# Spreading the rounding of the second MLP weights and stretching the first half of the first MLP chunk

## Chip, cores, metric

One core of a Trainium2 chip. The metric is the device time of one launch in microseconds (us); the median of several executions is given. TensorE is called PE, VectorE DVE, ScalarE ACT and GpSimd POOL, as in the profile.

## The reference

```
scores = q @ k.T / 8                       # 8 x 8 heads, 576 x 576, head size 64
thresh = max(scores, axis=-1) - 0.02
attn   = softmax(where(scores >= thresh, scores, -1e9))
x      = (attn @ v), heads side by side    # 4608 tokens x 512
out    = relu(x @ w_in)**2 @ w_out         # w_in 512 x 2048, w_out 2048 x 512
```

## The kernel before

Attention goes in 160 steps: a pair of heads and one block of 128 queries (the fifth block of a visit, the half block, has 64 queries of both heads). The MLP goes in 12 chunks of 384 tokens. A chunk's work waits in a queue and is dealt out between the attention's parts by a rate; its first half is 32 `mlp_in` parts, its second 24 `mlp_out` parts. The weights come as 64-bit floats and are rounded on the chip in 32 pieces: 0 to 15 are w_in, 16 to 31 w_out.

One piece passes three engines:

```python
        if stage == 0:      # ScalarE, twice
            nc.scalar.activation(out=e, in_=hi.bitcast(FP32), func=AF.Copy, scale=2.0 ** -112)
            nc.scalar.activation(out=d, in_=lo, func=AF.Copy, scale=2.0 ** -52)
        elif stage == 1:    # VectorE, lines 116, 117, 119
            nc.vector.tensor_scalar(out=tu, in0=hi, scalar1=0x80000000, ...)
            nc.vector.scalar_tensor_tensor(out=tu, in0=eu, scalar=3, in1=tu, ...)
            nc.vector.tensor_scalar(out=eu, in0=tu, scalar1=0xFF800000, ...)
        elif stage == 2:    # GpSimd, line 121
            nc.gpsimd.tensor_tensor(out=d, in0=d, in1=e, op=ALU.mult)
        else:               # GpSimd, line 123
            nc.gpsimd.tensor_tensor(out=weight_piece(i)[1], in0=t, in1=d, op=ALU.add)
```

The softmax's start has, after each pair of row maxima, three tiny operations of 128 x 2 elements:

```python
        for u in range(n):
            nc.vector.tensor_reduce(out=mx[:, u:u + 1], in_=sc[u][:, :, 0:HALF], ...)            # line 184
        nc.vector.tensor_scalar(out=bias, in0=mx, scalar1=-SCALE, scalar2=None, op0=ALU.mult)    # 185
        nc.vector.tensor_scalar(out=thr, in0=mx, scalar1=ntau8, scalar2=None, op0=ALU.add)       # 186
        nc.vector.tensor_tensor(out=z, in0=thr, in1=mx, op=ALU.is_gt)                            # 189
```

The loop (cut), with the rate and the table of pieces:

```python
    def rate(s):
        have = sum(x[0] for x in waiting)
        best = 1e9
        for e in sorted(chunk_at) + [NST + 2]:
            if e > s:
                best = min(best, have / (e - s))
                have += CHUNK_US * len(chunk_at.get(e, ()))
        return best
    ...
        if s <= min(chunk_at) - 2:                 # min(chunk_at) is 13
            x = int(visits[n][1].index(i) != 1)
        else:
            x = 1 if n < 2 * HP else 2
        pieces.append(min(x, left))
    ...
    for s in range(NST + 3):
            if now:
                round_weights(now[0], 0)
            scores(n, i)
            if now or early():
                exponents(n, i)
            if now:
                round_weights(now[0], 1)
                round_weights(now[0], 2)
            ...  # transposes of the next q and k, mix, a quarter of the MLP work
        for part in range(3):
            turn(*steps[s - 1], part)      # transposes of the last step's weights
            ...  # threshold after part 0, divide after part 1, a quarter of the MLP work
            if now:
                end_rounding(now[0])       # the add, and the load of the piece after next
            for p in now[1:]:              # a second piece: all of it here
                for stage in range(3):
                    round_weights(p, stage)
                end_rounding(p)
```

## Time and profile before

| | before |
|---|---|
| median, range (us) | 1628.0 (1627.86 to 1628.01), 3 executions |
| span of the profiled execution | 1625.4 |
| PE / DVE / POOL busy | 96% / 43% / 31% |

A stage's row in the profile gives its bounds, its length, the busy us and number of instructions of each engine, the clock that TensorE was granted (1.00 is full) and the DMA share. Everything from step 39 on is full of TensorE work, so what can be won or lost is TensorE's time before it: idle, or run at half clock.

### The profile page before, as it was taken

The page shows a single profiled execution, that of the slowest core. Times are in us where ns is not written, and L with a number is a line of the kernel's source. Part 1 is how long each engine was busy: PE and PEld are TensorE (multiplying, and loading weights), DVE is VectorE, ACT ScalarE, POOL GpSimd, SP SyncE. Part 2 cuts the span into 40 slices and gives each one's busy share as a digit, 9 for nine tenths or more (in the row PEclk, how much of TensorE's full clock was granted, in tenths as well). Part 3 has the DMA queues.
Part 4 walks back from the last instruction along what each step waited for, and adds up shares of the span by engine and source line. Part 5 has one row for each costly group of instructions (what it writes and reads, how often), then busy time and mean ns, then how long its engine had stood idle before and what let it go on. Part 6 is the DMA issues. An engine that isn't in the chain of part 4 may idle for free.

```text
span 1625.4 us, 18644 instructions
## 1 busy us (share of the span) xinstructions
PE 1561.2 (96%) x6464; PEld 851.8 (52%) x6464; DVE 696.0 (43%) x1833; ACT 556.3 (34%) x1157; POOL 503.6 (31%) x655
## 2 busy tenths in 40 slices
PE   5789779999999999999999999999999999999998
PEld 3455435555555455555555455555556455555453
DVE  6778994444344334444434344343434434320000
ACT  3555543333333233333333333233234233221010
POOL 4457771232232132132133133123124123212030
PEclk9889889999999999999999999999999999999999
DMA  6446330210210110120111110120111020000000
GB/s 149 93 111 145 91 83 7 57 23 7 48 32 7 35 23 1 35 51 1 35 29 23 35 29 0 35 44 8 29 35 22 7 57 1 14 13 0 20 1 20
DMA packets 224190, 59.29 MB, mean 36 GB/s; under 512 B 215392, under 2 KB 215392, under 8 KB 224096
## 3 DMA queue, kind: packets, MB, share of 16 engines
q1 hardware_dynamic: 224064, 58.10, 16.3%
q8 instruction: 52, 0.85, 0.2%
q14 instruction: 42, 0.34, 0.1%
q0 software_dynamic: 32, 0.00, 0.0%
HBM read 48.63 MB, written 9.44 MB: 36 GB/s over the span
## 4 chain that ended last, share of the span: by engine, by line
PE 89%; DVE 7%; SPq 1%; issue 1%; ACT 0%; POOL 0%; DMA 0%; DVEq 0%; ACTq 0%; POOLq 0%
PE o L286 30%; PE h L270 29%; PE s L180 11%; PE x_ps L254 10%; PE w_ps L227 7%; DVE st L184 2%; DVE w L207 2%; DVE cv L117 1%; PE w_ps L231 1%; SPq L136 1%; DVE cv L119 1%; DVE cv L116 1%; DVE st L185 1%; DVE st L186 0%; ACT w L196 0%
## 5 line engine op out<-in xcount | busy, mean ns | idle before, releaser
L270 PE MATMUL h<-xT,w_in_sb 128*128 128x384 f32 x1536 | 549.7, 493 | 0.0
L286 PE MATMUL o<-w_out_sb,g 128*128 128x512 f32 x1152 | 540.9, 599 | 0.0
L216 POOL TENSOR_SCALAR w<-w,st 128x576 f32<-128x576 f32 x288 | 238.0, 835 | 565.8 <-DVE st L210 550.2
L184 DVE TENSOR_REDUCE st<-s 128x1 f32<-128x576 f32 x288 | 206.8, 753 | 417.8 <-PE s L180 417.8
L207 DVE SCALAR_TENSOR_TENSOR w<-s,st,w 128x576 f32<-128x576 f32 x288 | 224.8, 814 | 315.9 <-ACT w L196 315.8
L270 PEld LDWEIGHTS h<-xT,w_in_sb 128*128 128x128 f32 x1536 | 271.6, 191 | 162.4 <-issue 30.8
L286 PEld LDWEIGHTS o<-w_out_sb,g 128*128 128x128 f32 x1152 | 200.9, 190 | 189.1 <-issue 187.7
L228 ACT COPY wT<-w_ps 128x384 f32<-128x384 f32 x384 | 180.8, 482 | 316.4 <-PE w_ps L227 315.4
L276 POOL TENSOR_TENSOR g<-r 128x384 f32<-128x384 f32 x192 | 159.6, 831 | 367.9 <-ACT r L274 366.6
L227 PEld LDWEIGHTS w_ps<-ident,w 128*128 128x128 f32 x1152 | 150.5, 145 | 157.1 <-issue 109.0
L180 PE MATMUL s<-kT,qT 64*128 64x288 f32 x1024 | 182.7, 448 | 41.8 <-DVE w L207 32.9
L196 ACT ACTIVATE w<-s,st 128x576 f32<-128x576 f32 x288 | 200.2, 745 | 56.7 <-DVE st L185 56.6
L227 PE MATMUL w_ps<-ident,w 128*128 128x128 f32 x1152 | 189.2, 282 | 14.1 <-ACT wT L228 10.3
L274 ACT ACTIVATE r<-h 128x384 f32<-128x384 f32 x192 | 94.4, 492 | 250.0 <-PE h L270 240.3
L254 PE MATMUL x_ps<-wT,vs 128*64 128x192 f32 (+1 forms) x1280 | 177.6, 426 | 0.0
L180 PEld LDWEIGHTS s<-kT,qT 64*128 64x128 f32 x1024 | 102.9, 194 | 131.3 <-issue 92.2
L254 PEld LDWEIGHTS x_ps<-wT,vs 128*64 128x64 f32 x1280 | 89.1, 142 | 82.9 <-issue 70.7
L257 ACT COPY xT<-x_ps 128x384 f32<-128x384 f32 (+1 forms) x64 | 25.4, 397 | 242.2 <-PE x_ps L254 242.2
L121 POOL TENSOR_TENSOR cv<-cv 128x512 f32<-128x512 f32 x32 | 40.7, 1273 | 53.3 <-DVE cv L119 45.2
L290 ACT COPY osb<-o 128x512 f32<-128x512 f32 x36 | 21.1, 586 | 104.0 <-PE o L286 101.8
L180 PE MATMUL s<-kT,qmid 128*128 128x288 f32 x128 | 38.5, 426 | 4.1 <-DVE w L207 4.1
L186 DVE TENSOR_SCALAR st<-st,ntau 128x2 f32<-128x2 f32 (+1 forms) x160 | 39.4, 246 | 0.0
(37 smaller groups left out, 504.0 us busy)
## 6 DMA issues: line engine op xcount, KB each, us to landing
ql<-in_q_dram SPq DMA_DIRECT2D x144, 72.0 KB, 2.7
kl<-in_k_dram SPq DMA_DIRECT2D x144, 72.0 KB, 2.7
vs<-in_v_dram SPq DMA_DIRECT2D x72, 128.0 KB, 2.5
out_dram<-osb SPq DMA_DIRECT2D x36, 256.0 KB, 2.1
area<-in_moe_w_in_dram SPq DMA_DIRECT2D x16, 512.0 KB, 4.1
area<-in_moe_w_out_dram SPq DMA_DIRECT2D x16, 512.0 KB, 3.7
vs<-in_v_dram SPq DMA_DIRECT2D x72, 16.0 KB, 2.4
ntau<-in_tau_dram POOLq DMA_DIRECT2D x1, 0.5 KB, 3.3
```

Of the source, the lines that this page charges most:

```text
L180: nc.tensor.matmul(sc[u][:, half, 0:HALF], lhsT, kT[rows, at:at + HALF], start=True, stop=True)
L184: nc.vector.tensor_reduce(out=mx[:, u:u + 1], in_=sc[u][:, :, 0:HALF], axis=AX.XY, op=ALU.max)
L196: nc.scalar.activation(out=w[:, u, :].rearrange("p (h k) -> p h k", h=2), in_=sc[u][:, :, 0:HALF], func=AF.Exp, bias=st[:, 1, u:u + 1], sc ...
L207: nc.vector.scalar_tensor_tensor(out=wu, in0=sc[u][:, :, 0:HALF], scalar=thr[:, u:u + 1], in1=wu, op0=ALU.is_ge, op1=ALU.mult, accum_out=s ...
L216: nc.gpsimd.tensor_scalar(out=w[:, u, :], in0=w[:, u, :], scalar1=z[:, u:u + 1], scalar2=rcp[:, u:u + 1], op0=ALU.add, op1=ALU.mult)
L227: nc.tensor.transpose(ps[:, n, :], w.rearrange("p u k -> p (u k)")[:, c * P:(c + 1) * P], ident)
L228: nc.scalar.copy(wT[:, 3 * part:3 * part + 3, cols], ps[:, 0:3, :])
L254: nc.tensor.matmul(ps[u * D:(u + 1) * D, 0:nq], vs[n % 2][:, u * (NBLK + 1) + c, :], wT[:, cw, cols], start=(c == 0), stop=(c == NBLK))
L270: nc.tensor.matmul(h, w_in_sb[:, c, f * P:(f + 1) * P], xT[:, c, at:at + TCH], start=(c == 0), stop=(c == NMC - 1))
L274: nc.scalar.activation(out=r, in_=h, func=AF.Relu)
L276: nc.gpsimd.tensor_tensor(out=gs[j, f], in0=r, in1=r, op=ALU.mult)
L286: nc.tensor.matmul(o, gs[j, f][:, t * P:(t + 1) * P], w_out_sb[:, f, :], start=(f == 0), stop=(f == NFT - 1))
```

## The change

Its intent: two pieces a step crowd VectorE in steps 20 to 27, so round one a step (two only in the half block), and slow the first half of chunk 0 so that its second half, which reads w_out, starts only when w_out is nearly rounded.

```diff
     def rate(s):
+        if s < out_from:
+            return sum(x[0] for x in waiting if x[1] is mlp_in) / (out_from - s)
         have = sum(x[0] for x in waiting)
@@
-            x = 1 if n < 2 * HP else 2
+            x = 2 if n >= 2 * HP and i == NBLK else 1
         pieces.append(min(x, left))
@@
+    out_from = next(s for s in range(NST) if sum(pieces[:s]) >= n_pieces - 2)
```

`out_from` comes out as 32.

## The prediction

> **What bounds the kernel now.** I read the busy table first, then the 40 slices, then the stretches around the MLP's first chunk, then the waits and single instructions inside the slow stretch.
>
> ```profile
> PE 1561.2 (96%) x6464; PEld 851.8 (52%) x6464; DVE 696.0 (43%) x1833; ACT 556.3 (34%) x1157; POOL 503.6 (31%) x655
> ...
> PE   5789779999999999999999999999999999999998
> ...
> DVE  6778994444344334444434344343434434320000
> ...
> POOL 4457771232232132132133133123124123212030
> PEclk9889889999999999999999999999999999999999
> ```
>
> TensorE is 96% busy, so nothing that only makes another engine cheaper can help after about 280 us (slice 7 on). The weak place is the first six or seven slices of 40.6 us: PE shows 7 in slices 4 and 5 (162 to 244 us) while DVE shows 9, and the clock is not full. That is where the second weights are rounded.
>
> I cut the trace at the first score matmul of chosen attention steps. There are 160 steps (pair of heads, block of queries); the first MLP chunk is admitted at step 13, the next at step 39. Step 13 begins at 99.66 us, step 20 at 150.68, step 28 at 233.14, step 39 at 311.99. The columns are length, busy us of the engines, PE clock, DMA share.
>
> ```profile
> core 0: us, PE busy (x) PEld busy (x) DVE busy (x) ACT busy (x) POOL busy (x), PEclk, DMA share, GB/s
> 99.66:150.68 51.02, 48.52 (x242) 29.17 (x242) 41.90 (x97) 27.64 (x61) 37.12 (x45) 0.96 0.63 143
> 150.68:233.14 82.46, 63.68 (x262) 35.35 (x263) 76.75 (x138) 41.62 (x84) 62.14 (x60) 0.88 0.43 105
> 233.14:311.99 78.85, 75.23 (x335) 39.90 (x334) 44.48 (x118) 28.86 (x61) 21.55 (x29) 0.97 0.08 19
> 311.99:1625.40 1313.41, 1309.22 (x5357) 706.61 (x5355) 462.02 (x1306) 413.50 (x869) 337.98 (x464) 1.00 0.11 23
> ```
>
> Steps 13-19 (one rounded piece each) take 7.3 us each, steps 20-27 (two pieces) 10.3, steps 28-38 (none) 7.2. In the second row DVE is 93% busy and PE 77%: VectorE bounds it. In the last row PE is 99.7% busy, and the change leaves that row's work alone. So only 212.3 us (51.0 + 82.5 + 78.9) are in play. The same stretch shows what two pieces a step do:
>
> ```profile
> ACT cv L113 <- POOL w_out_sb L123: 29.8, 7, 5.3
> ...
> PE w_ps L227 <- ACT wT L228: 10.3, 3, 4.1
> ...
> PE s L180 <- DVE w L207: 5.8, 4, 4.2
> ```
>
> ScalarE stands still seven times before the first conversion of a piece, because the two rounding buffers are still held by GpSimd; being in order, it then delivers its PSUM copies late, PE idles 3 to 4 us, and comes back slow:
>
> ```profile
> 187.48 0.90 PE L227 MATMUL w_ps<-ident,w 128*128 128x128 f32 x3 [4.11 <-ACT wT L228]
> 188.17 2.77 PE L270 MATMUL h<-xT,w_in_sb 128*128 128x384 f32 x4
> 190.74 2.13 PE L180 MATMUL s<-kT,qmid 128*128 128x288 f32 x4
> ...
> 196.19 1.56 PE L270 MATMUL h<-xT,w_in_sb 128*128 128x384 f32 x4
> ```
>
> The same four h matmuls take 2.77 us just after the idle 4.11 us, and 1.56 us (1.30 from start to start in a row of them) once warm.
>
> **What the Trainium skill says.** "TensorE: Matmul & The Clock Gate", Part 1 (the HAM clock gate): the array runs at half clock after an idle window of about 3.4 us and at full clock after a busy one. The trace agrees: 2.77 against 1.56 us above, and a mean clock of 0.88 in the second stretch. "SBUF — State Buffer", Who interferes with whom: VectorE and GpSimd share one pair of SBUF ports as an exclusive lock that some VectorE forms take, and the loser waits out the whole instruction. The trace agrees: the mask of a piece (line 116) takes 0.41 us alone but 1.50 us at 163.74, 175.49, 185.94, exactly beside GpSimd's 1.27 us multiply or add. I found no page needed for the DMA: the loads run four pieces ahead.
>
> **The change part by part.** No instruction is added or removed: 32 pieces, 768 + 576 MLP matmuls, the same attention. Only their places move.
>
> Rounding. Nine pieces are done before step 13 in both. Before, 7 in steps 13-19 and 16 in steps 20-27. After: 7 in 13-19; then one per step, two in the last block of a visit (steps 24 and 29), until the 23 are out in step 33. So 14 pieces in steps 20-31, 2 in 32-33.
>
> MLP. The 32 first-half pieces of chunk 0 (1.30 us of PE each) used to go out 17 in steps 13-19, 15 in 20-25, and its 24 second-half pieces (1.72 us each) in steps 26-38. Now the new rate spreads the first half evenly up to step 32: 12 pieces in 13-19, 20 in 20-31; then all 24 second-half pieces fall in 32-38, three or four per step. I followed the fill rule step by step for these counts. From step 39 both kernels stand alike within one piece.
>
> *Steps 13-19.* Same pieces on DVE, 5 fewer h parts, 6.5 us less on PE. But the loop here is score matmul, reduce, rounding, threshold, next score: for a full block, from reduce at 124.72 to the reciprocal's end at 130.70 is 6.0 us; a half block with its transposes 130.61 to 136.83, 6.2 us; and 0.93 to 1.28 us of waiting for PE per pair: 13.4 us per pair. Less PE work and a few less GpSimd squarings barely shorten it. 51.0 becomes 50.
>
> *Steps 20-31, now 12 steps.* A full block with one piece costs 6.0 us and a score round trip of about 1.0: 7.0. The step that transposes the next q and k adds 2 x 0.75: 8.5. The last block of a visit with two pieces: 6.2 - 1.5 + 2.3 = 7.0 on DVE, but PE has 1.1 of scores, 3.4 of mixing, some 2.1 of h and 1.15 of transposes, 7.7; so 7.7. Its second piece hides the next round trip, so block 0 after it costs 6.0. Steps 20-23: 7.0 + 8.5 + 7.0 + 7.0 = 29.5; 24-28: 7.7 + 6.0 + 8.5 + 7.0 + 7.0 = 36.2; 29-31: 7.7 + 6.0 + 8.5 = 22.2. Sum 87.9. I add 2 for cold spells: PE carries only 26 us of h and about 39 of attention here (72%), so idle spots of 1.5 to 2.5 us recur and some may drop the clock. 90.
>
> *Steps 32-38.* PE: 24 x 1.72 = 41.3, scores 8.1, transposes 7.5, mixing 3.4 + 1.8: 62.1, plus 2 for the first steps: 64. DVE's 7 x 4 us and two pieces lie beside it.
>
> Sum 50 + 90 + 64 = 204 against 212.3: a gain of 8. With the 1628.0 measured: 1620. The gain is small because VectorE's work is unchanged: the pieces cost 53.2 us of DVE in this stretch, 2.3 each, of which 2.1 or less is their own when no port is contested.
>
> **The rivals.** (a) *Nothing gained, or a little lost.* The work moved off PE in steps 13-31 must be done later, where PE is full: steps 32-38 cost 64 for 7 steps, against 50 (7 x 7.2) before, and VectorE's loop with a single piece leaves a hole at each round trip that a second piece used to fill. For it: steps 13-19 already run at 7.3 us with one piece and hold 3 us more h per pair than they will. If steps 20-31 cost 8.2 each and the clock drops often, 51 + 98 + 65 = 214: 1630. Against: the 7.3 include cold spells at step 13, which took 10.4 us.
> (b) *Full repair.* All stalls of two-piece steps vanish, contention halves, and steps 20-31 go at 6.5: 48 + 78 + 62 = 188, a gain of 24: 1604. For it: steps 28-38 before took 7.2 with more PE work. Against: DVE's own work in steps 13-31 is 127 us uncontended (13 full blocks of 4.33, 6 half of 2.69, 7 transposes of 1.5, 21 pieces of 2.1), and in steps 20-31 alone there remain the round trips.
> (c) *A late weight.* Second-half pieces start at step 32 with 30 pieces rounded; the last two rows are first read by the eighth piece, in step 34, a step after the last is rounded. I expect no wait. If each were a few us: 1625.
>
> **Range and chances.** Centre 1620; half of the weight within 5 us. Rival (a) gives the upper side, a mild form of (b) the lower: 1611 to 1629. Faster by over 2% needs 32.6 us out of 212; the PE work in it alone is about 168 (82 of MLP and 86 of attention at warm rates) and VectorE's bound leaves even less, so 0.02. Slower by over 2% would need steps 13-38 to average 9.4 us, 0.01. Within 2%: 0.97.
>
> **What would show it.** Of the profile after: step 20 begins at about 150, step 32 at about 240, step 39 at about 304, and from there to the end again 1313 us. DVE busy in steps 20-31 near 85%, not 93%; ScalarE's wait for GpSimd before line 113 shrinks from 29.8 us to under 5; PE idles of over 3 us in these steps fall from four to at most two; the line 116 mask's mean over the run drops below its 605 ns. I am wrong if step 32 begins after 248 (rival a, then look for idle PE before scores and a clock below 0.88) or before 230 (rival b), or if out matmuls wait for weights (rival c), or if the stretch from step 39 differs by more than 3 us.

## The result, and the profile after

| | before | after |
|---|---|---|
| median (us) | 1627.93 (1625.67 to 1628.01), 4 executions | 1624.26 (1623.77 to 1625.47), 4 executions |
| ratio after / before | | 0.9982, 95% interval 0.9965 to 0.9999 |

A ratio here is the mean time of one kernel's fast executions over the mean of the other's in the same rounds, so it is not quite the ratio of the medians. The unaltered changed kernel ran twice more on other occasions, with five rounds each: 1623.57 us, ratio 0.998 (0.9967 to 0.9994), and 1623.73 us, ratio 0.9981 (0.9967 to 0.9995). It is a gain of about 3 us where 8 were predicted: the direction was right, the size less than half. Measured by a bound of 2%, the two kernels count as the same, and so does every run below; what follows reads the 95% intervals.

The slices of the changed kernel:

```profile
PE   5788879999999999999999999999999999999999
...
DVE  6778775434444343444334344343434434320000
...
PEclk9789889999999999999999999999999999999999
```

The dip of TensorE is now an 8, 8, 8, 7 and longer; VectorE's two 9s are gone. The same stages, cut at steps 13, 20, 32 and 39:

```profile
core 0: us, PE busy (x) PEld busy (x) DVE busy (x) ACT busy (x) POOL busy (x), PEclk, DMA share, GB/s
99.41:150.31 50.90, 43.53 (x223) 26.19 (x223) 41.42 (x97) 27.27 (x59) 34.37 (x43) 0.93 0.60 138
150.31:248.15 97.84, 78.04 (x368) 46.08 (x368) 78.77 (x173) 50.17 (x103) 62.82 (x68) 0.88 0.38 91
248.15:310.60 62.45, 62.45 (x250) 31.46 (x250) 31.24 (x86) 22.27 (x45) 19.83 (x24) 1.00 0.11 23
310.60:1623.70 1313.10, 1309.18 (x5356) 706.69 (x5354) 461.18 (x1302) 413.27 (x868) 337.64 (x463) 1.00 0.11 23
```

In the kernel before, step 32 begins at 264.6 by the score matmuls of its trace, and its steps 20 to 31 were

```profile
150.68:264.61 113.93, 92.67 (x391) 50.42 (x392) 94.91 (x179) 51.80 (x106) 72.45 (x72) 0.90 0.32 79
```

The stages beside their predicted lengths:

| steps | before | predicted | after, first profile | second and third |
|---|---|---|---|---|
| 13 to 19 | 51.0 | 50 | 50.9 | 50.5, 50.7 |
| 20 to 31 | 113.9 | 90 | 97.8 | 95.2, 95.3 |
| 32 to 38 | 47.4 | 64 | 62.4 | 62.4, 62.2 |
| 39 to the end | 1313.4 | 1313 | 1313.1 | 1313.1, 1313.2 |

One stage is off, by 5 to 8 us. In the first profile it gained 16.1 us on before and steps 32 to 38 gave back 15.0: the net is a small difference of two large numbers, so an error of 6 to 9% in one of them takes more than half of it. The time up to step 13, where the change does nothing, was 99.4, 100.6 and 101.4 us in the three profiles, so single profiles are compared by stages here and not by their totals.

The waits in steps 20 to 31 of the changed kernel (us in total, times, longest):

```profile
ACT w L196 <- DVE st L185: 33.0, 12, 4.7
...
PE s L180 <- DVE w L207: 13.3, 5, 4.3
DVE st L184 <- PE s L180: 12.1, 10, 2.6
...
PE w_ps L227 <- ACT wT L228: 6.7, 4, 2.3
...
ACT cv L113 <- POOL w_out_sb L123: 2.3, 2, 1.5
```

The wait of ScalarE for the rounding buffers has shrunk from 29.8 to 2.3 us, as expected. But ScalarE's exponentials now wait 33.0 us for line 185, the tiny operation that makes their bias (4.7 us in the same steps before). Most of these 33.0 us are the wait for the scores and their maxima ahead of line 185: in a run below, where ScalarE makes the bias itself, it still waits 24.2 us for line 184. What line 185 itself was longer than undisturbed comes to 4.3 us. Here is one such place, in step 26, VectorE first and GpSimd second (start, length, what):

```profile
199.26 1.49 DVE L184 TENSOR_REDUCE st<-s 128x1 f32<-128x576 f32 x2 [1.31 <-PE s L180]
200.79 1.00 DVE L185 TENSOR_SCALAR st<-st 128x2 f32<-128x2 f32 x1
201.71 0.21 DVE L186 TENSOR_SCALAR st<-st,ntau 128x2 f32<-128x2 f32 x1
```

```profile
199.73 0.83 POOL L276 TENSOR_TENSOR g<-r 128x384 f32<-128x384 f32 x1
200.51 1.26 POOL L123 TENSOR_TENSOR w_out_sb<-cv 128x512 f32<-128x512 f32 x1
```

Line 185 takes 0.17 us undisturbed; here 1.00, and it ends when GpSimd's add of the last piece (200.51 + 1.26 = 201.77) does. What did not wait fits "SBUF — State Buffer", Who interferes with whom, in the Trainium skill: a VectorE instruction with two inputs in SBUF contends with a GpSimd instruction that reads SBUF, one with at most one such input (outside the two-port modes) does not. The threshold (line 207), with one input in PSUM and one in SBUF, kept its 0.81 us beside GpSimd's multiply (196.00 and 196.23), while line 209, with two SBUF inputs, took 1.28 instead of 0.16 us beside an add in a run below. And here is the passage after a pair, from step 24 to 26, VectorE and then TensorE:

```profile
189.40 1.83 DVE L117 SCALAR_TENSOR_TENSOR cv<-cv 128x512 uint32<-128x512 uint32 x1 [1.44 <-ACT cv L113]
...
193.39 1.10 DVE L189 TENSOR_TENSOR st<-st 128x2 f32<-128x2 f32 x1
```

```profile
191.31 1.46 PE L270 MATMUL h<-xT,w_in_sb 128*128 128x384 f32 x4
196.97 2.99 PE L180 MATMUL s<-kT,qT 64*128 64x288 f32 x8 [4.20 <-DVE w L207]
199.89 3.14 PE L254 MATMUL x_ps<-wT,vs 128*64 128x192 f32 x20
```

The second piece waits for ScalarE (1.44 us), then for GpSimd's port (1.83 instead of 0.69, beside an add from 189.42 to 190.68), so the next scores are reduced late. TensorE stands idle for 4.20 us and then works at a granted clock of 0.50 (197 to 200 us): 2.99 us for the scores instead of the 1.24 at 188.09.

A tally from the single instructions, as the sum of what each was longer than undisturbed (lines 185, 186, 189 and 209: 0.18, 0.22, 0.17, 0.17 us; 116, 117, 119: 0.42, 0.69, 0.43 us), steps 20 to 31:

| | pieces (116 to 119) | 185 + 186 + 189 | 209 | steps 20-31 |
|---|---|---|---|---|
| before | 14.6 | 10.9 | 1.6 | 113.9 |
| after | 3.3 | 7.4 | 2.6 | 97.8 |
| after, second profile | 3.2 | 8.4 | 2.6 | 95.2 |
| after, third profile | 3.2 | 10.3 | 2.6 | 95.3 |

The change freed the pieces from GpSimd's port, but the tiny operations kept most of their share. In steps 13 to 19, with 7 pieces, they were longer by only 1.0 to 1.5 us.

### The profile page after: what moved, and what is told of

Same layout as the page of the kernel before. It is cut to its first block, busy times and chain, and to the rows that moved or that the text cites. A ratio compares the mean times of both kernels' runs of the same rounds, so it can differ in the third digit from the quotient of the medians.

```text
span 1623.7 us, 18628 instructions
## 1 busy us (share of the span) xinstructions
PE 1558.0 (96%) x6464; PEld 851.8 (52%) x6464; DVE 682.3 (42%) x1833; ACT 557.8 (34%) x1157; POOL 499.6 (31%) x655
## 4 chain that ended last, share of the span: by engine, by line
PE 91%; DVE 6%; SPq 1%; issue 1%; ACT 1%; DMA 0%; POOL 0%; DVEq 0%; ACTq 0%; POOLq 0%
PE o L286 31%; PE h L270 30%; PE s L180 12%; PE x_ps L254 10%; PE w_ps L227 7%; DVE st L184 2%; DVE cv L117 1%; DVE w L207 1%; PE w_ps L231 1%; SPq L136 1%; DVE cv L119 1%; DVE cv L116 0%; DVE st L185 0%; ACT w L196 0%; DVE st L189 0%
## 5 line engine op out<-in xcount | busy, mean ns | idle before, releaser
L257 ACT COPY xT<-x_ps 128x384 f32<-128x384 f32 (+1 forms) x64 | 25.5, 399 | 245.8 <-PE x_ps L254 245.8
L234 ACT COPY wT<-w_ps 128x256 f32<-128x256 f32 x64 | 20.7, 376 | 60.1 <-PE w_ps L231 60.1
```

## The experiments

Four theories of why steps 20 to 31 take 95 to 98 us and not 90. **P** (port lock): GpSimd's add of a piece falls on the start of the next step and holds up the tiny operations in front of the exponentials. **D** (dear pairs): the second piece in steps 24 and 29 costs more than its own 2.1 us. **C** (clock): the half clock after idle spots is what costs. **R** (ring): the third group of transposes waits for ScalarE's copy of the first, which stands behind the exponentials. All sixteen runs gave correct results. Each ran five rounds beside the kernel before on the same chip; the profile is of one of the five. The runs were on four chips, and the unaltered changed kernel ran on two of them only, so runs on different chips are compared by their ratios to the kernel before. Two executions of the changed kernel differed by 2.7 us in steps 20 to 31, so a difference of that size in one profile shows nothing.

### A third buffer for the transposes (theory R)

```diff
-        ps = psum.tile([P, 4, P], FP32, tag="mm" if early() and part == 1 else "tx", ...)
+        ps = psum.tile([P, 4, P], FP32, tag="mm" if state["step"] < out_from and part == 1 else "tx", ...)
```

> The changed kernel, but in the steps before the second half may start (13 to 31) the second group of transposes goes to the MLP's PSUM buffers instead of the transposes' own two, so that the third group need not wait for ScalarE's copy of the first, which stands behind this step's exponentials. Theory R (a ring: scores, reduce, exponentials, copy, third transposes, h, next scores, closed by that wait): steps 20 to 31 fall from 97.8 us to about 90, the total from 1624 to about 1617. Theory C (the half clock after idle times is what costs) expects about 1623, since the idle time only moves before the scores. Theory D (the two-piece steps 24 and 29 are what costs): 1624, with the idle 4.2 us before steps 26 and 31 still there.

Measured 1625.47 us, ratio 0.9987 (0.9975 to 1.0); steps 20 to 31 took 96.6 us. That is no gain: R falls, for the edit did remove TensorE's wait of these transposes for ScalarE's copies (line 227 for line 228, 6.7 us in 4 waits; none is left in the trace). The wait of the exponentials stayed, with 30.2 us in that stage:

```profile
ACT w L196 <- DVE st L185: 30.2, 12, 4.8
```

### Never more than one piece a step (theory D)

```diff
-            x = 2 if n >= 2 * HP and i == NBLK else 1
+            x = 1
```

> The changed kernel with never more than one piece a step; rounding then ends in step 35 and the second half starts at step 34. Theory D (two-piece steps): the idle 4.2 us of TensorE after steps 24 and 29 goes, 3 to 6 us gained: about 1620. Theory R (ring): every step has the ring, so the stretch up to step 34 keeps 8 us a step and the total stays at 1624 or rises to 1626.

Measured 1629.76 us, ratio 1.0017 (1.0005 to 1.003): slower, so by the total D seems to fall. The stages say otherwise:

```profile
core 0: us, PE busy (x) PEld busy (x) DVE busy (x) ACT busy (x) POOL busy (x), PEclk, DMA share, GB/s
148.70:239.70 91.00, 76.13 (x361) 44.20 (x361) 73.96 (x170) 46.89 (x96) 57.71 (x64) 0.91 0.40 100
239.70:302.80 63.10, 58.08 (x237) 29.83 (x237) 34.36 (x89) 25.06 (x50) 25.78 (x29) 0.97 0.10 22
302.80:1626.60 1323.80, 1319.62 (x5380) 710.80 (x5378) 459.20 (x1302) 412.47 (x868) 337.48 (x462) 1.00 0.11 23
```

Steps 20 to 31 fell to 91.0 with two pieces fewer, and step 39 began at 302.8. But the second half, which could start only at step 34, no longer fitted before step 39: 6 of its 24 parts came after, and 6 x 1.72 = 10.3 us of TensorE's time is nearly all that the last stage grew by (1323.8 against 1313.1). Steps 32 and 33 in turn had little for TensorE to do. The stage is 4.2 to 6.8 us shorter for two pieces fewer, and steps 25 and 30, the blocks after the former pairs, fell from 16.5 us together to 11.4 (step bounds by the first score matmul). So a second piece costs about 2.5 us there, instead of being hidden, and this run paid for its absence elsewhere. (The first half was also stretched two steps further, so the run has two changes.)

### The two halves of the change alone

The stretched rate with the old pieces:

```diff
-            x = 2 if n >= 2 * HP and i == NBLK else 1
+            x = 1 if n < 2 * HP else 2
...
-    out_from = next(s for s in range(NST) if sum(pieces[:s]) >= n_pieces - 2)
+    out_from = 32
```

> The stretched rate alone: the first half of chunk 0 spread up to step 32, but the pieces as before, two a step from step 20 to 27. If the gain of the change comes from the thinner rounding, this gives none: steps 20 to 27 stay at 82 us, steps 28 to 31 fall to about 26 to 28 (little work), 32 to 38 take 62.5: 51 + 82 + 27 + 62.5 = 222, about 10 us slower than before: 1637. If the gain comes from moving MLP work out of the crowded steps, steps 20 to 27 shorten by some 5 us, total 1625 to 1630.

Measured 1636.24 us, ratio 1.0059 (1.0046 to 1.0072); steps 20 to 31 took 107.4 us and 32 to 38 62.9. Almost as expected from "none of the gain" (steps 20 to 27 took 78.6 us, not 82): VectorE is busy for 95.13 of those 107.4 us, and TensorE's work is only put off.

The spread pieces, with the first half at its old pace and the second half still held until step 32:

```diff
-            return sum(x[0] for x in waiting if x[1] is mlp_in) / (out_from - s)
+            return min(3.15, sum(x[0] for x in waiting if x[1] is mlp_in))
```

> The thinner rounding with the first half at its old pace (3.15 us of MLP a step, done at step 25), then no MLP work until step 32. If the stretch is bound by VectorE and the ring, the place of the MLP parts matters little: steps 13 to 31 together as in the changed kernel within 3 us, total 1622 to 1627. If a full TensorE (clock) is what counts, steps 13 to 25 speed up and 26 to 31 slow down by the clock; total 1626 to 1632.

Measured 1622.94 us, ratio 0.9978 (0.9964 to 0.9992): the same as the whole change. Steps 13 to 19 took 50.9 and 20 to 31 95.4 us. So the gain is the spreading's (with the second half held back until step 32 in both); how the first half is dealt out beneath it makes no measured difference, even with a mean clock of 0.86:

```profile
150.50:245.90 95.40, 76.52 (x348) 44.12 (x348) 79.63 (x173) 49.78 (x102) 62.58 (x67) 0.86 0.37 91
```

### Idle work to keep TensorE warm (theory C)

```diff
+        if min(chunk_at) < s < out_from:
+            warm = psum.tile([P, 512], FP32, tag="mm", name="warm", bufs=2)
+            for c in range(2):
+                nc.tensor.matmul(warm[:, 0:TCH], ident, w_in_sb[:, c, 0:TCH], start=True, stop=True)
         if on:
             if now:
                 end_rounding(now[0])
```

> The changed kernel with 1.3 us of idle work for TensorE (two float32 matmuls that nobody reads) at the end of each of steps 14 to 31. Theory C (half clock after idle times, 12.6 us more of TensorE's busy time in steps 20 to 31 than its warm rates make): the clock there rises from 0.88 to above 0.97 and the steps shorten by 3 to 6 us in spite of 15 us more work: total 1619 to 1621. Theories P and D: the added work delays the scores in the tight steps: steps 20 to 31 become 0 to 6 us longer, total 1624 to 1630.

```profile
150.40:251.20 100.80, 88.75 (x416) 51.44 (x415) 78.26 (x171) 50.70 (x105) 62.34 (x68) 0.97 0.34 85
```

Measured 1629.88 us, ratio 1.002 (1.0007 to 1.0032). The clock did rise to 0.97, but steps 20 to 31 became longer, 100.8 us. A warm TensorE bought this way is worth less than the time it costs. Whether the half clock by itself costs a few us is not settled by this run, since the idle work also stands in front of the scores. But the mean clock of the stage does not go with its length: 0.88, 0.91 and 0.93 in the three profiles of the changed kernel with 97.8, 95.2 and 95.3 us, and 0.86 with 95.4 in the run above.

### Exponentials after the first copy (theory R again)

```diff
-            if now or early():
+            if early():
                 exponents(n, i)
...
-                if not (now or early()):
+                if not early():
                     exponents(n, i)
```

> The changed kernel with the exponentials of steps 12 to 33 behind the copy of the first transposes on ScalarE, as they already are in steps without a piece. Theory R (copies stuck behind exponentials close a ring), already weak after the third buffer moved the total by nothing: 3 us or more gained. Theory P: the exponentials and with them the threshold come later, since the first transposes themselves wait for GpSimd's division: total unchanged or up to 8 us worse, 1624 to 1632.

Measured 1625.4 us, ratio 0.9993 (0.998 to 1.0005); steps 20 to 31 96.5 us. No gain: R stays fallen. (The edit moves them in steps 13 to 33; in step 12 `early()` still holds.)

### The add of a piece right after its multiply (theory P)

```diff
             if now:
                 round_weights(now[0], 1)
                 round_weights(now[0], 2)
+                end_rounding(now[0])
...
-            if now:
-                end_rounding(now[0])
             for p in now[1:]:
```

> The changed kernel with GpSimd's closing add of a piece (line 123) issued right after its multiply (line 121) and not at the end of the step. Theory P (port lock): the add falls on the start of the next step, where VectorE's tiny operations on the row maxima wait for it, in front of the exponentials; in steps 20 to 31 they are 10.0 us longer than their undisturbed times. Moved, the stretch of those falls to under 4 us and steps 20 to 31 from 97.8 to about 90 us; total about 1617 (0.993 to 0.995 of the kernel before). Theory C (half clock): at most 2 us gained. Theory D (two-piece steps): at most 1 us.

Measured 1622.11 us, ratio 0.9968 (0.9956 to 0.9981). Steps 20 to 31 took 91.1 us, as expected, but steps 13 to 19 went from 50.9 to 53.5 (in that profile), so the total was above the expected 1617. The stretch of lines 185, 186 and 189 fell from 7.4 to 4.9 us, not to under 4, and line 209's rose from 2.6 to 6.5: part of the lock moved behind the threshold.

The unaltered changed kernel as the scale:

> The changed kernel unaltered, on this chip and in these rounds, as the scale for the other three: 0.997 to 0.9995 of the kernel before, 1623 to 1625.

Measured 1623.57 us, ratio 0.998.

The same with the old order kept up to step 19:

```diff
                 round_weights(now[0], 2)
+                if s >= 20:
+                    end_rounding(now[0])
...
-            if now:
+            if now and s < 20:
                 end_rounding(now[0])
```

> As the kernel with GpSimd's add right after its multiply, but only from step 20, since in steps 13 to 19 that run lost 2.6 us. Theory P: steps 13 to 19 at 51, steps 20 to 31 at 91: total 1619 to 1620, ratio 0.9955 to 0.9965. If the first run's 91 was chance: 95 to 98 again and a ratio of 0.998.

Measured 1620.51 us, ratio 0.9961 (0.9948 to 0.9973): the ratio is within what P expected, the total just above it.

```profile
150.20:242.00 91.80, 77.29 (x367) 45.36 (x367) 78.34 (x174) 50.62 (x103) 64.42 (x67) 0.91 0.39 94
```

Step 27, whose line 186 waited in the changed kernel, shows where the lock is now:

```profile
206.24 0.17 DVE L185 TENSOR_SCALAR st<-st 128x2 f32<-128x2 f32 x1
...
209.84 1.28 DVE L209 SCALAR_TENSOR_TENSOR st<-st 128x2 f32<-128x2 f32 x1
```

Line 185 is back at 0.17 us; line 209 waits instead, for the add that runs from 209.82 to 211.09. Of the later work only GpSimd's division needs line 209's result; the next scores need the threshold ahead of it. The wait is not free, though: VectorE's next row maximum follows at 211.23 without idle time between.

### More of the lock (theory P, the other way)

```diff
-                round_weights(now[0], 2)
+                if not 20 <= s < 32:
+                    round_weights(now[0], 2)
...
             if now:
+                if 20 <= s < 32:
+                    round_weights(now[0], 2)
                 end_rounding(now[0])
```

> The dose the other way: in steps 20 to 31 GpSimd's multiply of a piece (1.27 us) is moved to the end of the step too, in front of its add, so that twice as much GpSimd work can fall on the start of the next step. Theory P (port lock in front of the exponentials): the stretch of the three tiny operations ahead of the threshold rises from 7.4 us to 12 or more, steps 20 to 31 lengthen by 4 to 10 us, total 1627 to 1633. If the place of GpSimd's work matters only through the sum of its time: unchanged, 1624.

Measured 1632.25 us, ratio 1.0033 (1.002 to 1.0045), beside 0.9981 for the changed kernel on the same chip. The three tiny operations were longer by 16.0 us in sum and not by 10.3 (the third profile of the changed kernel), and steps 20 to 31 took

```profile
152.00:256.10 104.10, 80.37 (x367) 46.98 (x367) 91.43 (x173) 50.42 (x103) 63.76 (x67) 0.87 0.33 83
```

against 95.3. GpSimd's busy time is nearly the same (63.76 and 62.72 us): it is where its work lies that costs. This supports the port lock as the cause of lost time, but not the tiny operations alone: the pieces' own instructions (lines 116 to 119) were longer by 9.1 us, not 3.2, and ScalarE waited 6.6 us for the rounding buffers.

### The left-over pairs where TensorE is the bound (theory D)

```diff
-            x = 2 if n >= 2 * HP and i == NBLK else 1
+            x = 1 if s < 32 else 2
...
+    out_from = 32
```

> The changed kernel with one piece a step up to step 31 and the two left-over pairs in steps 32 and 33, where TensorE's second half is the bound and VectorE has room; the second half still starts at step 32. The run with never more than one piece showed steps 20 to 31 at 91.0 us for 12 pieces against 95 to 98 for 14. Theory D (a second piece inside the stretch costs more than its 2.1 us): steps 20 to 31 at 91, 32 to 38 at 62 to 64: total 1617 to 1619, ratio 0.994 to 0.9955. Theory P alone (port lock, in every step): 2 x 2.1 us at most: total 1620, ratio 0.9965.

Measured 1622.18 us, ratio 0.9967 (0.9954 to 0.9981): nearer to what P alone expected.

```profile
149.60:243.10 93.50, 78.71 (x369) 46.16 (x369) 73.57 (x170) 47.95 (x99) 57.14 (x65) 0.89 0.40 95
```

Steps 32 to 38 took 64.0 us, so 2 to 4 us were won and 1.6 given back.

### The bias on ScalarE (theory P)

```diff
-        nc.vector.tensor_scalar(out=bias, in0=mx, scalar1=-SCALE, scalar2=None, op0=ALU.mult)
+        if min(chunk_at) <= state["step"] < out_from:
+            nc.scalar.activation(out=bias, in_=mx, func=AF.Copy, scale=-SCALE)
+        else:
+            nc.vector.tensor_scalar(out=bias, in0=mx, scalar1=-SCALE, scalar2=None, op0=ALU.mult)
```

> The changed kernel with the bias of the exponentials made by ScalarE from the row maxima in steps 13 to 31, and not by VectorE's tiny operation (line 185), which there waited for GpSimd's port by 4.3 us in sum. Theory P: the exponentials no longer wait for GpSimd; the other tiny operations still do, but beside them: steps 20 to 31 shorten by 3 to 5 us, total 1619 to 1621, ratio 0.9955 to 0.997. If the exponentials are not on the path there, 0 to 1 us: ratio 0.998.

Measured 1621.43 us, ratio 0.9966 (0.9953 to 0.9978). The total is near P's range, but steps 20 to 31 took 94.8 us in the profile, no clear gain; alone it stays open. Lines 186 and 189 still waited (8.1 us in sum), beside the exponentials now.

### Together

All three edits (pairs in steps 32 and 33, add early from step 20, bias on ScalarE):

> All three together: left-over pairs in steps 32 and 33, bias on ScalarE, add right after the multiply from step 20. If the costs of pairs and of the port lock are separate: steps 20 to 31 at 84 to 87, total 1612 to 1614, ratio 0.991 to 0.9925. If they are one and the same wait: no better than the best of the three, about 1617.

Measured **1614.47 us, ratio 0.9929 (0.9916 to 0.9941)**: faster than both kernels by intervals clear of theirs, though by less than 2%.

```profile
148.10:235.20 87.10, 74.11 (x369) 42.69 (x369) 73.21 (x158) 50.31 (x111) 59.94 (x66) 0.96 0.39 99
235.20:298.90 63.70, 62.64 (x250) 30.97 (x250) 36.96 (x88) 24.57 (x49) 24.18 (x27) 1.00 0.10 23
298.90:1612.20 1313.30, 1309.14 (x5356) 706.66 (x5354) 461.33 (x1302) 413.28 (x868) 336.45 (x463) 1.00 0.11 23
```

Without the bias:

> Pairs in steps 32 and 33, and the add right after the multiply from step 20, the bias still on VectorE. If the bias on ScalarE added nothing of its own: as the kernel with all three, steps 20 to 31 at 87 to 88, ratio 0.992 to 0.9935. If it added its own 2 us: ratio 0.994 to 0.995.

Measured 1616.64 us, ratio 0.9941 (0.9928 to 0.9953):

```profile
149.10:236.90 87.80, 73.54 (x367) 42.64 (x367) 74.68 (x167) 47.75 (x99) 58.10 (x62) 0.96 0.40 101
```

Without the early add:

> Pairs in steps 32 and 33, and the bias on ScalarE, the add still at the end of the step. If the add's place is the larger of the two: steps 20 to 31 at 91 to 93, ratio 0.9955 to 0.997. If freeing the bias alone is as good as moving the add: 87 to 88, ratio 0.992 to 0.9935.

Measured 1617.28 us, ratio 0.9942 (0.9929 to 0.9954):

```profile
149.50:237.80 88.30, 76.72 (x367) 45.16 (x367) 73.17 (x155) 50.74 (x111) 57.56 (x64) 0.92 0.39 98
```

This is nearly the better of the two cases. The sum of the tiny operations' waits did not fall (7.4 us, and 6.7 with the pairs alone moved); only line 185's went, from 4.4 to nothing, and the stage is 5.2 us shorter than with the pairs alone moved. That is the most direct sign that the wait ahead of the exponentials is what counts, but no proof: it is one profile of each on two chips, the intervals of the ratios touch (0.9942 and 0.9967), and with the pairs in place the same edit showed no clear gain. The last scale run:

> The changed kernel unaltered once more, as the scale for these three: ratio 0.997 to 0.9995, steps 20 to 31 at 95 to 98.

Measured 1623.73 us, ratio 0.9981. So on one chip, removing the pairs and either cure of the lock gives 0.994, and the unaltered change 0.998, with intervals clear of each other. The two cures gain the same, probably because both take GpSimd's add out of the bias's way (line 185 was longer by 2.2 us with the add early, by 4.4 with the pairs alone moved). Whether having both is better than one (0.9929 against 0.9941) is within the intervals.

## Why the prediction was right or wrong

**The bound and the ledger: right.** Only the 212 us from step 13 to 38 changed; the stage from step 39 took 1313.1 us (1313.4 before). The total of 1624 us lies inside the stated range of 1611 to 1629; what failed is the size of the gain, 3 us for 8.

**Steps 13 to 19 ("barely shorten it", 50): right**, 50.5 to 50.9, although TensorE had 5.0 us less busy time there.

**Steps 32 to 38 (64): right**, 62.4, with TensorE never idle. No out matmul waited for a weight (rival c did not occur).

**Steps 20 to 31 ("Sum 87.9. I add 2 for cold spells ... 90"): the step that failed**; 97.8, 95.2 and 95.3 were measured, between the 90 and rival (a)'s 98. Rival (a)'s sign, step 32 beginning after 248, came in once, barely (248.15), and not in the other two profiles (246.24, 247.36). Cut at each step's first score matmul, and set beside the terms of the sum (us), two terms were too small:

| steps | term of the sum | predicted | changed kernel, three profiles | add early from 20 | pairs moved | both |
|---|---|---|---|---|---|---|
| 25, 30: block 0 after a pair | 2 x 6.0 | 12.0 | 16.5, 16.5, 16.5 | 15.0 | 11.4 | 11.4 |
| 24, 29: last block, with a pair | 2 x 7.7 | 15.4 | 15.4, 15.4, 15.4 | 15.4 | 15.4 | 15.4 |
| 21, 26, 31: with the next q and k | 3 x 8.5 | 25.5 | 28.0, 28.0, 26.6 | 27.0 | 28.2 | 26.7 |
| 20, 22, 23, 27, 28: other full blocks | 5 x 7.0 | 35.0 | 37.9, 35.3, 36.8 | 34.5 | 38.4 | 34.3 |
| all | | 87.9 | 97.8, 95.2, 95.3 | 91.8 | 93.5 | 87.8 |

- The first, the same in every profile: "Its second piece hides the next round trip, so block 0 after it costs 6.0". Steps 25 and 30 took 8.9 and 7.7 us, 4.5 more than the predicted 12.0. The second piece waited for ScalarE and then for the port. With the pairs out of there, the same blocks took 5.7 us each: there was no hole for the second piece to fill, and it cost about 2.5 us each time. The trace before held a hint: steps 14 and 16, which follow a half block with one piece, took 5.8 us each.
- The second, 2.8 to 5.4 us over eight steps: "A full block with one piece costs 6.0 us". It was taken from steps 13 to 19, where a full block is followed by a half block. There GpSimd's add ran beside the row maxima (125.06 to 126.32), which did not wait, and the 6.0 includes a wait of 0.55 us on line 209. In a run of full blocks the add lands on the next block's lines 185 to 189, ahead of the exponentials; these were longer by 7.4 to 10.3 us in sum, and with the add moved the eight steps took 61.5 us in place of 63.3 to 65.9 (60.5 predicted). I had seen such a lock in the pieces and expected it to go; I did not ask what else used the port at that time. The trace before showed it: line 186 took 1.32 instead of 0.22 us at 162.30, 174.06 and 184.50, just ahead of each line 116 that I quoted.

Moving the add alone took 3.5 us off the third profile's 95.3, moving the pairs alone 1.8, both 7.5. The 1.8 alone would be within the spread of 2.7 us, and so is the difference between 7.5 and the sum of the parts; the 7.5 is not, and the totals bear it out (0.994 against 0.998). With both, the stage took 87.8 us, the sum before its 2 us for cold spells, though with 12 pieces in it and not 14.

**The side signs.** Line 116's mean fell from 605 to 457 ns; ScalarE's wait for the buffers fell to 2.3 us; idle spots of over 3 us in TensorE fell to two (4.20 and 4.31): all as said, except that there were five such spots before (3.24, 3.03, 4.11, 4.18, 3.13), not four. VectorE's busy share in steps 20 to 31 was 80.5% (78.77 of 97.84), not the predicted 85%, which is the same miss seen from the other side. A piece's own time was also misread: uncontested it is 0.42 + 0.69 + 0.43 = 1.54 us of VectorE, not 2.1. Taken alone that would have made the stage shorter, so it does not explain the miss.

**The clock.** I allowed 2 us for cold spells. The clock was 0.88 to 0.93 there. Raising it to 0.97 by idle work did not help the total, and the stage's length does not go with it; it went to 0.96 by itself once the add and the pairs were moved. What the half clock costs by itself stays open.

## What to carry to other kernels

In a program that is full of one engine's work from some point on, the total is that work plus what the engine loses before it; add up the losses by stage, because a change that moves work often gains in one stage and gives back in the next. A duration taken from one place holds only for the same neighbours: ask for each stage which engine shares a port with the short instructions at the head of the chain, and place the other engine's long work behind them. Do not count work as hidden in a hole before the trace shows the hole. Left-over work of a second engine belongs where the first engine is the bound (here in steps 32 and 33), not where the second is.

## What the Trainium skill lacked or had wrong

- "SBUF — State Buffer", Who interferes with whom, says that the loser waits out the whole instruction; this case agrees (line 185: 1.00 us instead of 0.17, ending with GpSimd's 1.26 us add). What it does not spell out is that a tiny loser waits as long as a large one: in the changed kernel's profile a 128 x 2 operation was longer by up to 1.10 us (line 186, 1.32 instead of 0.22) and a 128 x 512 one by up to 1.15 (line 116, 1.57 instead of 0.42), so tiny operations at the head of a chain are worth a look first.
- "TensorE: Matmul & The Clock Gate", Part 1, speaks of an idle window of about 3.4 us before the clock halves. Here an idle spot of only 2.30 us (before the transposes at 219.79 us of the changed kernel) stood before a halved clock: the granted clock was 1.00 from 215.2 to 217.4 us and 0.50 from 219.8 to 222.5, with matmuls of 2.73 us in place of 1.46. The page's remark in "A second HAM failure mode", that frequent short idling makes the clock swing, is nearer to this; no page gives the share of idle time that does it.
